# Half-height tiles for the scores and the carried products of a gated linear attention: two accumulated 64-row halves in place of one 128-row product

## The chip, the cores and the metric

The kernel runs on one core of a Trainium2 chip. A core has a matrix engine (TensorE, PE in the profile), which multiplies a loaded tile of weights by a streamed operand and adds into PSUM banks; three engines that work on rows of memory (VectorE or DVE, ScalarE or ACT, GpSimd or POOL); and a sync engine (SP) that issues most of the DMAs. Each engine runs its own stream of instructions in order and waits on semaphores for the others. The metric is device time in microseconds (us) from start to end of one execution.

## The reference

For 4 batches of 8 heads, 768 positions and 48 channels, a complex, data-dependent decay moves a 48x48 state; the real part of the state, read by the query, is the output. An ELU feed-forward layer follows.

```python
mag = np.sqrt(a_re * a_re + a_im * a_im)
scale = np.minimum(mag, 0.999) / (mag + 1e-06)
ar, ai = a_re * scale, a_im * scale
for t in range(S):
    S_re, S_im = ar * S_re - ai * S_im + k_t v_t, ar * S_im + ai * S_re
    y[:, :, t] = einsum('bhd,bhde->bhe', q[:, :, t], S_re)
x = y.transpose(0, 2, 1, 3).reshape(B * S, H * D)      # 3072 x 384
h = x @ w_in                                           # 384 x 2048
g = where(h > 0, h, exp(min(h, 0)) - 1)
out = g @ w_out                                        # 2048 x 384
```

## The kernel before, in words

The 3072 positions are cut into twelve steps `u` = 0 to 11. Each step takes 128 positions of two batches (`NB` = 2, index `n`), and each 128 positions are two chunks of 64 (`C` = 128, `L` = 64, index `c`). Complex numbers are written into one column of 128 rows: rows 0 to 47 hold the real part, rows 64 to 111 the imaginary part, and the rest is zero (`HP` = 64). So one product over 128 rows adds real and imaginary terms at once.

For a step of `u` > 2 the attention on PE stands in two places of a fixed list.

- The first place, `small` with what follows it: the state products (`state_products`, L1075: keys by values, for batch 0), the scores (L1190: transposed keys `kt` by transposed queries `qt`, for each head `h`, batch `n` and chunk `c`), and the state products of batch 1. Scores go into two PSUM banks `x["t"][n]`, which a mask on DVE (`masked`, L1198) brings to memory as `a`. DVE adds each state product to the old state (L1090), and POOL multiplies it by the decay (L1092), which makes the new state `S`. The step's first place in the list is `r + 28.2`, with `r` = 16 list slots per step.
- The second place, `valued_pe` and `carried_pe` at `r + 31.3`: values (`value_products`, L1111: `a` by `vn`), the sums of the next step's decays (`quartered`, L900), and the carried products (`carried_products`, L1120: state `S` by `qt`), all into two banks `x["yy"][c]`. ACT copies them (`copied`, L1228 and L1231), POOL's DMAs move a few rows (`seam`, L1241), and the feed-forward layer of that step starts from `x`.

Between and after them PE works on the feed-forward layer: L1507 (first layer, `mult`) and L1370 (second layer, `product`), from step 3 on in fast bilinear forms. Steps 0 to 2 have a list of their own (`first`); for step 2 the functions `scored` and `valued` do the work.

PE's tiles: a product whose weights span 128 rows and 64 or 48 columns (L1190, L1120) occupies half of the array's columns, and two of them run side by side. One of 64 rows and 64 columns (L1075, L1111, L900) occupies a quarter, and four run side by side. Everything else uses the whole array. Every float32 multiplication of the program runs as two passes, each a weight load and a matmul, so one product of the program is four instructions of PE; a transpose (L1034) is one pass.

What sets the order: the plan is a list of (place, function) pairs, sorted once. `put` adds to each place an offset from the table `SHIFT`, by function, arguments and step. Within an engine the instructions keep that order; semaphores are put in wherever one engine's data are another's. Buffers matter at two points: the banks of `outs()` (`y0`, `y1`, one buffer each) serve the feed-forward layer, the scores and the values in turn; and the three `w` banks serve the state products, the decay sums and the transposes in turn.

Of the kernel before, what the change touches and what calls it, by code (L numbers as in the profile page):

```python
# [16 lines left out]
C = 128  # L17
L = 64
# [487 lines left out]
def kernel(  # L506
# [600 lines left out]
    def value_products(u, n, y, first=True, at=0):  # L1107
        x = nat[u]
        for p, c, j in EACH:

            nc.tensor.matmul(  # L1111
                y[c][ts(j, HP), ds(at + p * L, L)], lhsT=vn[u % 2][ts(c, L), n, ds((2 * p + j) * D, HP)],
                rhs=x["a", n][ts(c, L), 2 * p + j], start=(first and p == 0), stop=False,
                skip_group_check=True,
            )
# [22 lines left out]

    def scored(u):

        x = nat[u]
        t = outs()
        state_products(u, 0 if u > PAIRED else 1)
# [7 lines left out]
        if u > PAIRED:  # L1151
            state_products(u, 1)
        for n in range(NB):
            state_sums(u, 0 if u > PAIRED else 1, [n])
            x["a", n] = new("a", 2, [C, H, L])
            nc.vector.tensor_tensor(
                out=x["a", n], in0=t[n].rearrange("p (h t) -> p h t", h=H),
                in1=mask.unsqueeze(1).to_broadcast([C, H, L]), op=ALU.mult,
            )
        if u > PAIRED:  # L1160
            state_sums(u, 1)

    def valued(u):

        x = nat[u]
        y = outs()
        for n in range(NB):
            value_products(u, n, y, n == 0, n * NP * L)
        if u + 1 < NU:
            both = quartered(u + 1)  # L1170
        for n in range(NB):
            carried_products(u, n, y, n * NP * L)
        if u == PAIRED:
            copied(u, y)
        if u + 1 < NU:
            z = nat[u + 1]
            z["E"], z["F"] = new("n", 6), new("n", 6)
            quarters_used(u + 1, both)
        if u > PAIRED:
            copied(u, y)  # L1180

    def small(u):

        x = nat[u]
        x["t"] = t = outs()
        state_products(u, 0)
        for n in range(NB):
            for h in range(H):
                for c in range(C // L):
                    nc.tensor.matmul(  # L1190
                        t[n][ts(c, L), ts(h, L)], lhsT=x["kt", n][:, h, ts(c, L)],
                        rhs=x["qt", n][:, h, ts(c, L)], start=True, stop=True,
                    )
# [9 lines left out]
    def valued_pe(u):  # L1203
# [4 lines left out]
        if u + 1 < NU:  # L1208
            x["quartered"] = quartered(u + 1)

    def carried_pe(u):
        for n in range(NB):
            carried_products(u, n, nat[u]["yy"], n * NP * L)
# [391 lines left out]
    def warm(n):  # L1605
# [42 lines left out]
    }  # L1648
# [26 lines left out]
    def gates_of(u, *at):  # L1675
# [23 lines left out]
        (convert,), (table, "trig_and_small", 1), (convert,), (seam, 0), (convert,), (warm, 1),  # L1699
# [12 lines left out]
        (inner, 1, 12), (load_a, 3), *2 * [(convert,)], (inner, 1, 8), (fetch, "out", 4),  # L1712
        (inner, 0, 10), (inner, 0, 14), (elu, 1, 12), (inner, 0, 12), (convert,), (fetch, "out", 5),
        *3 * [(convert,)], (load_v, 2), (powers, 2), (elu, 1, 8), *2 * [(convert,)], (elu, 0, 10),
# [168 lines left out]
```

## Time and profile before

| | |
|---|---|
| three runs | 644.2, 644.64, 646.19 us; median 644.64 us |
| the profiled execution | 644.48 us, of which the profiled span is 642.8 us |
| PE matmuls | busy 628.7 us (98%), 7236 of them |
| PE weight loads | 576.0 us (90%) |
| DVE, ACT, POOL | 489.3 us (76%), 428.5 us (67%), 159.0 us (25%) |
| scores of the steps 3 to 11 (L1190) | 576 matmuls of 128 rows and 64 columns |
| carried products (L1120) | 704 matmuls of 128 rows and 48 columns |
| one step, from state product to state product | 181.84 to 230.92: 49.1 us |

A row of the timeline gives the start, the time from first start to last end, the engine, the line, the operation, the tiles, the weights' rows and columns, the result's shape, and how many were merged. Matmuls overlap, so the difference of two starts says how long a run kept PE, and the second column is longer than that by the last one's own duration of about 0.22 us. "idle before" is time in which that engine did nothing, with what ended it; "issue" stands where no semaphore did. In the view of transfers, the 40 numbers behind GB/s are the bytes of 40 equal slices of the window, and a single packet shows in the slice in which it starts.

### The profile page before, as it was taken

How to read it: one execution, taken by the hardware profiler on the slowest of the kernel's cores; microseconds unless marked ns; L12 is line 12 of the kernel's file. 1: busy time of each engine (PE TensorE's matmuls, PEld its weight loads, DVE VectorE, ACT ScalarE, POOL GpSimd, SP SyncE). 2: the span in 40 equal slices, each digit the busy share in tenths (PEclk: the TensorE clock that was granted, in tenths of full speed). 3: DMA queues.
4: the chain of work that ended last, by engine and by line, in shares of the span. 5: the costliest groups of instructions: out<-in, count | busy, mean ns of one | idle time of the engine just before them, and what ended most of it. 6: DMA issues, size and time to landing. Idle time of an engine off the chain costs nothing.

```text
span 642.8 us, 17116 instructions
## 1 busy us (share of the span) xinstructions
PE 628.7 (98%) x7236; PEld 576.0 (90%) x7236; DVE 489.3 (76%) x777; ACT 428.5 (67%) x707; POOL 159.0 (25%) x201
## 2 busy tenths in 40 slices
PE   8899999999999999999999999999999999999996
PEld 5788886677899999999999999999999999999995
DVE  5899999869688698698488588588688678664581
ACT  5985573865957777677776776775876776771250
POOL 2000100113124315414414414413604502402000
PEclk9899999999999999999999999999999999999999
DMA  9967569325500712624434244243523352112100
GB/s 182 192 126 135 121 182 205 100 58 87 94 2 16 158 35 73 130 55 97 89 73 96 69 85 100 59 91 96 103 59 82 68 107 64 37 35 62 37 2 31
DMA packets 150706, 56.11 MB, mean 87 GB/s; under 512 B 128948, under 2 KB 142428, under 8 KB 150620
## 3 DMA queue, kind: packets, MB, share of 16 engines
q1 hardware_dynamic: 146880, 53.57, 38.3%
q0 software_dynamic: 3520, 1.20, 1.6%
q8 instruction: 59, 0.97, 0.6%
q14 instruction: 27, 0.22, 0.1%
q10 hardware_dynamic: 220, 0.14, 0.1%
HBM read 48.91 MB, written 4.80 MB: 84 GB/s over the span
## 4 chain that ended last, share of the span: by engine, by line
PE 95%; ACT 2%; DVE 1%; issue 1%; POOL 0%; DVEq 0%; ACTq 0%; POOLq 0%
PE mlp L1370 29%; PE mlp L1507 16%; PE mlp L1261 10%; PE y L1507 9%; PE w L1034 6%; PE w L1075 4%; PE y L1286 3%; PE mlp L1286 3%; PE y L1120 3%; PE y L1190 3%; PE w L848 2%; PE y L1111 2%; PE mlp L1609 1%; PE w L900 1%; PE w L1042 1%
## 5 line engine op out<-in xcount | busy, mean ns | idle before, releaser
L1370 PE MATMUL mlp<-w_out,g 128*128 128x192 f32 x640 | 112.1, 328 | 0.0
L1370 PEld LDWEIGHTS mlp<-w_out,g 128*128 128x128 f32 x640 | 104.3, 190 | 3.4 <-DVE ee L1384 0.6
L1092 POOL TENSOR_TENSOR S<-S,T 128x384 f32<-128x384 f32 x36 | 34.0, 946 | 204.9 <-DVE S L1090 204.9
L1523 DVE TENSOR_TENSOR g<-g,mlp 128x512 f32<-128x512 f32 x45 | 30.9, 686 | 48.9 <-PE mlp L1507 20.8
L1261 PE MATMUL mlp<-x,w_in 128*128 128x256 f32 x288 | 63.8, 380 | 0.0
L1261 PEld LDWEIGHTS mlp<-x,w_in 128*128 128x128 f32 x288 | 54.3, 190 | 8.2
L1348 DVE TENSOR_TENSOR g<-g 128x512 f32<-128x512 f32 x80 | 55.1, 703 | 5.0 <-PE mlp L1370 3.2
L1507 PE MATMUL mlp<-x,w_in 128*128 128x128 f32 x424 | 56.1, 275 | 0.0
L1370 PE MATMUL mlp<-w,g 128*128 128x192 f32 x320 | 54.5, 329 | 0.0
L1370 PEld LDWEIGHTS mlp<-w,g 128*128 128x128 f32 x320 | 51.8, 190 | 0.6
L1507 PEld LDWEIGHTS mlp<-x,w_in 128*128 128x128 f32 x424 | 51.6, 192 | 0.1
L1528 ACT ACTIVATE ee<-g 128x512 f32<-128x512 f32 x63 | 39.5, 626 | 18.2 <-DVE g L1523 16.8
L1241 POOL DMA_DIRECT2D x<-y x62 | 30.6, 501 | 75.8 <-ACT y L1137 39.9
L1532 DVE SCALAR_TENSOR_TENSOR g<-ee,g 128x512 f32<-128x512 f32 x63 | 43.5, 691 | 7.3 <-ACT ee L1529 7.1
L1529 ACT ACTIVATE ee<-ee 128x512 f32<-128x512 f32 x72 | 45.4, 631 | 2.3
L1520 ACT COPY g<-mlp 128x512 f32<-128x512 f32 x36 | 21.1, 586 | 37.5 <-PE mlp L1507 37.4
L1035 ACT COPY qt<-w 128x512 f32<-128x512 f32 x48 | 25.7, 593 | 8.6 <-PE w L1034 8.4
L1251 ACT ACT_TABLE_LOAD x24 | 30.8, 1283 | 0.5
L915 ACT ACTIVATE n<-w 64x384 f32<-64x384 f32 (+1 forms) x60 | 28.1, 486 | 3.9 <-PE w L900 3.0
L1507 PE MATMUL mlp<-x,g 128*128 128x128 f32 x224 | 29.6, 275 | 0.0
L1228 ACT COPY x<-y 128x384 f32<-128x384 f32 x20 | 8.6, 482 | 31.4 <-PE y L1120 31.4
L1507 PE MATMUL y<-x,w_in 128*128 128x128 f32 x216 | 28.6, 275 | 0.0
(226 smaller groups left out, 1416.6 us busy)
## 6 DMA issues: line engine op xcount, KB each, us to landing
w<-in_moe_w_out_dram SPq DMA_DIRECT2D x8, 768.0 KB, 4.7
g<-in_moe_w_in_dram SPq DMA_DIRECT2D x24, 256.0 KB, 3.1
g<-in_moe_w_out_dram SPq DMA_DIRECT2D x24, 256.0 KB, 2.7
w<-in_moe_w_in_dram SPq DMA_DIRECT2D x16, 288.0 KB, 4.0
vn<-in_v_dram SPq DMA_DIRECT2D x24, 192.0 KB, 4.1
q<-in_q_dram SPq DMA_DIRECT2D x11, 384.0 KB, 4.9
k<-in_k_dram SPq DMA_DIRECT2D x11, 384.0 KB
out_dram<-o SPq DMA_DIRECT2D x44, 96.0 KB, 2.4
```

Of the source, the lines that this page charges most:

```text
L1034: nc.tensor.transpose(t[:, h], of, ident)
L1092: eng.tensor_tensor(out=new_s, in0=new_s, in1=wide, op=ALU.mult)
L1251: nc.scalar.preload_act_table_set(name)
L1261: nc.tensor.matmul(t[:, e], lhsT=w_in[:, i, ts(f + e, C)], rhs=x["x"][:, i], start=(i == 0), stop=(i == NI - 1),)
L1286: nc.tensor.matmul(x["o", n], lhsT=x["g", f // 8][:, f % 8, ts(n, C)], rhs=w_out[:, f], start=(f == 0), stop=(f == NF - 1),)
L1348: nc.vector.tensor_tensor(out=S_of(u, k, h), in0=a, in1=b, op=op)
L1370: nc.tensor.matmul(to, lhsT=a[:, m], rhs=b[:, m], start=(first and h == 0 and m == 0), stop=False, skip_group_check=True,)
L1507: nc.tensor.matmul(x["c" + c][:, ts(m, C)], lhsT=a[:, m], rhs=x["mix"][p], start=(p == BANKS[c][0] and m == 0), stop=False, skip_group_che ...
L1523: nc.vector.tensor_tensor(out=part(u, to), in0=part(u, a), in1=part(u, b), op=op)
L1528: nc.scalar.activation(out=e, in_=part(u, of), func=AF.Relu, scale=-1.0)
L1529: nc.scalar.activation(out=e, in_=e, func=AF.Exp, scale=-1.0)
L1532: nc.vector.scalar_tensor_tensor(out=part(u, to), in0=nat[u]["e", to], scalar=-1.0, in1=part(u, of), op0=ALU.add, op1=ALU.max,)
```

## The change

Scores and carried products of 128 rows become two products of 64 rows each, which add into the same PSUM place: first one half of the rows (for the one batch or chunk the real rows, for the other the imaginary ones), later the other half. With 64 rows and 64 or 48 columns, four stand in the four quarters of the array. Both halves of one product add into one place of PSUM from different rows of the array, and the second is made to wait for the first: a POOL copy of a few elements of an operand onto themselves (`touched`) depends on every PE read of the first half, and the second half depends on it. Other PE work stands between the halves: the state products of batch 0 between those of the scores, the decay sums `quartered` between those of the carried products. The carried products of the steps 2 and 11, and the scores of the steps 0 to 2, stay whole.

```diff
+    def touched(t):
+        nc.gpsimd.tensor_copy(out=t, in_=t)
+
+    def score_half(u, m):
+        x = nat[u]
+        for h in range(H):
+            for n in (range(NB), (1, 0))[m]:
+                rows = ts(n ^ m, HP)
+                for c in range(C // L):
+                    nc.tensor.matmul(
+                        x["t"][n][ts(c, L), ts(h, L)], lhsT=x["kt", n][rows, h, ts(c, L)],
+                        rhs=x["qt", n][rows, h, ts(c, L)], start=(m == 0 and h == 0),
+                        stop=False, skip_group_check=True,
+                    )
+        if m == 0:
+            touched(x["kt", 1][:, 0 :: H - 1, 0::L])
+
+    def carried_half(u, m):
+        x = nat[u]
+        for n in (range(NB), (1, 0))[m]:
+            for p in range(NP):
+                for c in (range(C // L), (1, 0))[m]:
+                    for j in range(2):
+                        rows, h = ts(c ^ m, HP), 2 * p + j
+                        nc.tensor.matmul(
+                            x["yy"][c][ds(j * HP, D), ds((n * NP + p) * L, L)],
+                            lhsT=x["S", n][c][rows, h], rhs=x["qt", n][rows, h, ts(c, L)],
+                            start=False, stop=False, skip_group_check=True,
+                        )
+        if m == 0:
+            touched(x["S", 1][1][:, 0 :: H - 1, 0:1])
     def small(u):
         x = nat[u]
-        x["t"] = t = outs()
+        x["t"] = outs()
+        score_half(u, 0)
         state_products(u, 0)
-        for n in range(NB):
-            for h in range(H):
-                for c in range(C // L):
-                    nc.tensor.matmul(
-                        t[n][ts(c, L), ts(h, L)], lhsT=x["kt", n][:, h, ts(c, L)],
-                        rhs=x["qt", n][:, h, ts(c, L)], start=True, stop=True,
-                    )
+        score_half(u, 1)
     def valued_pe(u):
...
-        if u + 1 < NU:
-            x["quartered"] = quartered(u + 1)
-
-    def carried_pe(u):
-        for n in range(NB):
-            carried_products(u, n, nat[u]["yy"], n * NP * L)
+        if u + 1 == NU or u == PAIRED:
+            if u == PAIRED:
+                x["quartered"] = quartered(u + 1)
+            for n in range(NB):
+                carried_products(u, n, x["yy"], n * NP * L)
+            return
+        carried_half(u, 0)
+        x["quartered"] = quartered(u + 1)
+        carried_half(u, 1)
...
-        "state_sums(0, (1,))@3": 0.4, "state_sums(0, (1,))@4": -0.8, "state_sums(1, (1,))": 0.9,
-        "state_sums(1, (1,))@3": 0.5, "state_sums(1, (1,))@4": 2.0, "state_sums(1, (1,))@5": 0.2,
+        "state_sums(0, (1,))@3": 0.4, "state_sums(0, (1,))@4": -0.8, "state_sums(1, (1,))": 0.1,
...
-            for n in range(NB):
-                put(r + 28.2, state_sums, u, 1, (n,))
+            put(r + 28.2, state_sums, u, 1, (0,))
             put(at, valued_pe, u)
-            put(at, carried_pe, u)
+            put(at, state_sums, u, 1, (1,))
```

Some twenty more offsets of `SHIFT` and a few entries of the list `first` change; they move single operations of DVE and ACT by one or two places, and on PE one group of key transposes by four first-layer products, in the steps 6 to 11.

On PE, at the scores of step 3, this stands before (each row is a line of the program, the tiles' names, the result's columns of weights by streamed columns, and a count of the program's products; `vn`, `kg` are values and gated keys, `w` and `y` PSUM banks, `kt` and `cs` the transposed keys of batch 0 and 1):

```order
L1370 MATMUL mlp<-w_out,g 128x192 x4
L1075 MATMUL w<-vn_73,kg 64x48 x32
L1190 MATMUL y_1823<-qt,kt 64x64 x16
L1190 MATMUL y_1824<-qt,cs 64x64 x16
L1075 MATMUL w<-vn_73,kg 64x48 x32
L1370 MATMUL mlp<-w_out,g 128x192 x4
```

and this in the changed kernel, at the join of the first half, the state products and the second half:

```order
L1149 MATMUL y_1823<-qt,kt 64x64 x2
L1149 MATMUL y_1824<-qt,cs 64x64 x2
L1075 MATMUL w<-vn_73,kg 64x48 x32
L1149 MATMUL y_1824<-qt,cs 64x64 x2
L1149 MATMUL y_1823<-qt,kt 64x64 x2
```

The 32 score products have become 64, of which 32 stand ahead of the state products of batch 0 and 32 behind them; each half alternates between the two banks, two products at a time. The second state products (`L1075 ... x32`) and the feed-forward products follow as before.

At the carried products of step 3, PE had

```order
L1111 MATMUL y_1987<-a,vn_73 64x64 x2
L900 MATMUL w<-n,sum_logs 64x384 x4
L1120 MATMUL y_1986<-qt,S 48x64 x2
L1120 MATMUL y_1987<-qt,S 48x64 x2
```

and has now, from the last values over the end of the first half to the start of the second:

```order
L1110 MATMUL y_2017<-a,vn_73 64x64 x2
L1165 MATMUL y_2016<-qt,S 48x64 x2
...
L1165 MATMUL y_2017<-qt,S 48x64 x2
L900 MATMUL w<-n,sum_logs 64x384 x4
L1165 MATMUL y_2017<-qt,S 48x64 x2
```

Again 32 products are 64, half of them ahead of the decay sums.

On POOL, around one of the later steps, this stood before (L727, L1014 and L993 prepare the next step, L1092 multiplies a state, the DMAs L831 and L1241 move the carry and the seam):

```order
L727 TENSOR_TENSOR n<-n 128x768
L1092 TENSOR_TENSOR S<-S,T_77 128x384 x3
L831 DMA n<-carry 1x16x48
L1092 TENSOR_TENSOR S<-S,T_77 128x384
L1241 DMA x<-y 16x256 x6
```

and now:

```order
L727 TENSOR_TENSOR n<-n 128x768
L1140 COPY cs<-cs 128x2x2
L1092 TENSOR_TENSOR S<-S,T_77 128x384 x2
L831 DMA n<-carry 1x16x48
L1092 TENSOR_TENSOR S<-S,T_77 128x384
L1140 COPY S<-S 128x2
L1251 DMA x<-y 16x256 x6
L1092 TENSOR_TENSOR S<-S,T_77 128x384
```

The two copies of `touched` are new, and the fourth state multiplication now stands behind the DMAs of the seam. The line numbers of the changed kernel are higher by up to ten from L1140 on; L1507 and L1370 are L1517 and L1380 there.

More of the change, by code (lines that the diff above doesn't have):

```diff
@@ L1717 @@
-        (convert,), (fetch, "out", 6), (project, 1, 0, 0, 4), (convert,), (inner, 1, 14),
-        (slopes, 2), *3 * [(convert,)], (project, 1, 1, 0, 4), (project, 0, 0, 0, 4), (angles, 2),
-        (lengths, 2), (fetch, "out", 7), (convert,), (project, 0, 0, 4, 8), (elu, 1, 14),
-        (project, 0, 1, 0, 4), (decays, 2), (convert,), (project, 1, 0, 4, 8), (carried, 2),
-        (convert,), (table, "trig_and_small", 2), *2 * [(convert,)], (turns, 2), (waves, 2),
-        (scaled, 2), (convert,), (table, "natural_log_exp_and_others", 2), (project, 0, 1, 4, 8),
@@ L1729 @@
-        (project, 1, 0, 12, 16), (slopes, 3), (convert,), (transposed, 2, "q", 0),
-        (project, 1, 1, 12, 16), (angles, 3), (scored, 2), (opened,), (states, 2, 0), (valued, 2),
-        *3 * [(convert,)], (seam, 2), (project, 0, 0, 8, 12), (combined, 1, 1), (summed_in, 0),
-        (noted, 3), (carried, 3), (summed_in, 1), (combined, 2, 1), (combined, 1, 0),
-        (summed_in, 2), (project, 0, 1, 12, 16), (combined, 2, 0), (turns, 3), (combined, 4, 1),
-        (combined, 4, 0), (inner, 2, 4), (inner, 2, 6), (ends, 3), (load_a, 4), (inner, 2, 2),
@@ L1741 @@
[L1741 removed]
+        (inner, 1, 12), (load_a, 3), (convert,), (inner, 0, 10), (convert,), (inner, 1, 8),
+        (fetch, "out", 4), (inner, 0, 12), (inner, 0, 14), (elu, 1, 12), (convert,),
+        (fetch, "out", 5), *3 * [(convert,)], (load_v, 2), (powers, 2), (elu, 1, 8),
+        *2 * [(convert,)], (elu, 0, 10), (convert,), (noted, 2), (ratios, 2), *3 * [(convert,)],
+        (elu, 0, 14), (inner, 1, 10), *2 * [(convert,)], (elu, 0, 12), (convert,), (elu, 1, 10),
@@ new lines @@
+        *4 * [(convert,)], (load_qk, 2), (convert,), (fetch, "out", 6), (project, 1, 0, 0, 4),
+        (convert,), (inner, 1, 14), (slopes, 2), *3 * [(convert,)], (project, 1, 1, 0, 4),
+        (project, 0, 0, 0, 4), (angles, 2), (lengths, 2), (fetch, "out", 7), (convert,),
+        (project, 0, 0, 4, 8), (elu, 1, 14), (project, 0, 1, 0, 4), (decays, 2), (convert,),
+        (project, 1, 0, 4, 8), (carried, 2), (convert,), (table, "trig_and_small", 2),
+        *2 * [(convert,)], (turns, 2), (waves, 2), (scaled, 2), (convert,),
@@ new lines @@
+        (convert,), (ratios, 3), (convert,), (lengths, 3), (project, 1, 0, 12, 16), (slopes, 3),
+        (convert,), (transposed, 2, "q", 0), (project, 1, 1, 12, 16), (angles, 3), (scored, 2),
+        (opened,), (states, 2, 0), (valued, 2), *3 * [(convert,)], (seam, 2),
+        (project, 0, 0, 8, 12), (combined, 1, 1), (summed_in, 0), (noted, 3), (carried, 3),
+        (summed_in, 1), (combined, 2, 1), (combined, 1, 0), (summed_in, 2), (project, 0, 1, 12, 16),
+        (combined, 2, 0), (turns, 3), (combined, 4, 1), (combined, 4, 0), (inner, 2, 4),
```

69 lines of the change are left out of this document (22 added, 47 removed), and 36 rows, old and new, of the table SHIFT.

## The prediction

> **What bounds the kernel now.** The page comes first.
>
> ```profile
> span 642.8 us, 17116 instructions
> PE 628.7 (98%) x7236; PEld 576.0 (90%) x7236; DVE 489.3 (76%) x777; ACT 428.5 (67%) x707; POOL 159.0 (25%) x201
> q8 instruction: 59, 0.97, 0.6%
> PE 95%; ACT 2%; DVE 1%; issue 1%; POOL 0%; DVEq 0%; ACTq 0%; POOLq 0%
> ```
>
> The chain that ended last is PE for 95% of the span. The view of stretches says whether PE ever waits in the steps 3 to 11, which alone are changed:
>
> ```profile
> 170.00:590.00 420.00, 420.00 (x5400) 403.61 (x5399) 320.40 (x528) 299.81 (x487) 138.29 (x145) 1.00 0.34 76
> 181.84:231.00 49.16, 49.16 (x641) 47.33 (x644) 39.99 (x66) 35.10 (x56) 17.36 (x18) 1.00 0.30 63
> ```
>
> PE (first number behind the length) is busy for all of 420 us at clock 1.00. So a nanosecond taken off PE's stream comes off the end, and one that PE loses is lost. A step is 49.1 us and some 640 matmuls, with as many weight loads: 1280 instructions.
>
> The page's row q8 (packets, MB, share) is the third thing to see. 0.97 MB in 59 packets are 16 KB each, and 2 x 7236 PE instructions over 59 packets are 245, with PE's separate semaphore instructions about 256 of 64 bytes. These packets are PE's own instructions on their way in: five per step.
>
> **What the change removes: changes of tile shape.** The timeline of PE in step 3, and then in step 10:
>
> ```profile
> 181.84 1.15 PE L1075 MATMUL w<-vn,kg 64*64 64x48 f32 x64
> 182.92 1.15 PE L1190 MATMUL y<-qt,kt 128*64 128x64 f32 x32
> 183.90 1.10 PE L1190 MATMUL y<-qt,cs 128*64 128x64 f32 x32
> 184.93 1.15 PE L1075 MATMUL w<-vn,kg 64*64 64x48 f32 x64
> 186.01 1.57 PE L1370 MATMUL mlp<-w_out,g 128*128 128x192 f32 x8
> 192.71 1.16 PE L1111 MATMUL y<-a,vn 64*64 64x64 f32 x64
> 193.69 0.83 PE L900 MATMUL w<-n,sum_logs 64*64 64x384 f32 x8
> 194.45 1.99 PE L1120 MATMUL y<-qt,S 128*48 128x64 f32 x64
> 196.37 3.84 PE L1370 MATMUL mlp<-w,g 128*128 128x192 f32 x22
> 525.64 2.07 PE L1075 MATMUL w<-vn,kg 64*64 64x48 f32 x64
> 527.64 1.15 PE L1190 MATMUL y<-qt,kt 128*64 128x64 f32 x32
> 529.65 0.59 PE L1370 MATMUL mlp<-w_out,g 128*128 128x192 f32 x2
> ```
>
> Halving the rows gains nothing by itself. 64 passes of 128 rows in pairs are 32 turns; 128 passes of 64 rows in fours are 32 turns too. A turn costs the same: step 10's state products use two quarters, so 64 passes are 32 turns, 2.00 us (525.64 to 527.64); step 3's are 16 turns, 1.08 us. Sixteen turns are the difference, 0.92; I use 0.93, since the scores' 32 turns with both changes of shape take 2.01. Entering from a full tile and leaving without a change costs 0.98 (192.71 to 193.69), so a way in is about 0.05 and a way out 0.10.
>
> Scores, steps 3 to 9: before 186.01 - 181.84 = 4.17. After, four runs of 16 turns in one shape: 0.98 + 0.93 + 0.93 + 0.93 + 0.10 = 3.87. **-0.30 each, -2.1 for seven.** Steps 10 and 11 have both state products ahead and one change fewer: 529.65 - 525.64 = 4.01 against 3.87, **-0.14 each, -0.3**.
>
> Carried products, steps 3 to 10: before 196.37 - 192.71 = 3.66. After: values 0.98, first half (1.92 - 0.15)/2 = 0.89, decay sums without their change 0.76 - 0.10 = 0.66, second half with the way out 0.99: 3.52. At the 64-column turn of 0.93 the halves would give 3.60. **-0.14 each (-0.06 at least), -1.1 for eight.** All three: **-3.5 us**.
>
> **What it adds: instructions that PE must be fed with.** Each step gets 64 products more, 256 instructions, and the places where they stand are the densest. Before, 384 instructions took 4.17 us there; after, 512 would take 3.87. Whether PE gets them so fast is answered by step 2, where PE ran in small tiles for longest. Its timeline, with one row of step 1:
>
> ```profile
> 60.82 1.14 PE L1075 MATMUL w<-vn,kg 64*64 64x48 f32 x62
> 62.98 0.31 PE L1075 MATMUL w<-vn,kg 64*64 64x48 f32 x2 [1.02 <-issue]
> 138.78 1.15 PE L1147 MATMUL y<-qt,kt 128*64 128x64 f32 x32
> 140.80 1.36 PE L1075 MATMUL w<-vn,kg 64*64 64x48 f32 x61
> 142.04 1.06 PE L1111 MATMUL y<-a,vn 64*64 64x64 f32 x60
> 143.74 0.65 PE L1120 MATMUL y<-qt,S 128*48 128x64 f32 x16
> 145.14 1.55 PE L1120 MATMUL y<-qt,S 128*48 128x64 f32 x48 [0.75 <-issue]
> ```
>
> PE stopped for 1.02 and 0.75 us in the middle of runs, at products that wait for no semaphore. The run at 140.80 is longer than its like at 181.84 (1.36 with three passes still out, against 1.15); it halts behind 24 of its 64 passes, until 141.42. From there to the halt before 145.14 are 40 passes, 64 values, 8 sums and 16 carried ones: 128 matmuls, 256 instructions, one packet. Counted along the order, the halt of 62.98 lies on the same grid. The transfers around it, and those of step 3's scores (window from 181.84, slices of 0.15 us):
>
> ```profile
> GB/s 0 0 0 73 82 297 31 0 0 7 7 10 3 137 287 14 0 0 0 73 0 0 0 0 0 0 0 0 0 0 0 0 0 0 0 0 73 0 0 0
> q8 instruction: 3, 0.05, 2.4%
> GB/s 0 0 0 0 0 0 0 109 0 0 0 0 0 0 0 0 0 0 0 0 0 0 0 0 0 0 0 0 0 0 109 0 0 0 0 0 0 0 0 0
> q8 instruction: 2, 0.03, 2.3%
> ```
>
> In the first window (138 to 147, slices of 0.225) the three lone 73s are packets, at 138.8, 142.4 and 146.2. Each of the first two is followed by a halt that ends 2.6 to 2.7 us after its start (141.42, 145.14), and the next packet starts about one us after that. So in a dense stretch one packet follows another after some 3.6 us, and its 256 instructions are fed no faster than that.
>
> Now step 3. Its packets start at 182.9 and 186.4. On the grid (1024 instructions behind the halt of 141.42) the next boundary lies 36 passes into the second state products, 64 + 64 + 36 = 164 passes from the run's start: before at 1.08 + 2.01 + 0.04 + 0.52 = 3.65, so at 185.5, 2.6 behind the packet, and PE just does not halt. In step 6 the same distance is 2.4 (packet 330.4, boundary 332.8). With 1280 instructions per step, and 1536 after the change, five and six whole packets, the boundary stays at that place in every step.
>
> After the change the same 164 passes take 0.98 + 0.93 + 36/64 of 0.93 = 2.43. The packet cannot start sooner than before: what precedes it runs at the same pace, 1.07 after the run's start. Its instructions run 2.2 to 2.6 us after that (below step 6's 2.4, up to step 2's 2.6); I take 2.4, so 3.47. **PE halts for 1.04 us (0.8 to 1.25) in each of the steps 3 to 9: +7.3.** In step 10 the boundary lies 5 + 160 passes in, at 3.4, the packet 1.5 behind the start (527.1), so the halt is 0.5. In step 11 the boundary falls into L1370, which consumes two instructions in 0.16 us, and costs nothing. The values and carried halves hold one boundary, 123 passes in; the one before it was crossed in L1370, so that packet has long been there.
>
> The sum: 644.48 of the profiled execution - 3.5 + 7.3 + 0.5 = **648.8 us**, or 4.3 (0.7%) more. With the bounds of the halt and of the carried halves: 647.0 to 651.0. The median of the runs shown is 0.16 above the profiled execution, which is left out.
>
> [...]
>
> **What is hidden.** The copy of `touched` on POOL was not in the trace; its nearest rows are a 48x48 copy and a 128x128 product, beside the rows of the work around it in step 6:
>
> ```profile
> L1586 POOL COPY pair<-ident 48x48 f32<-48x48 f32 x2 | 0.4, 216 | 0.1
> L1490 POOL TENSOR_TENSOR x<-x 128x128 f32<-128x128 f32 x9 | 4.4, 488 | 33.6 <-DVE pair L1487 30.4 <-PE mlp L1507 3.2
> 331.47 0.83 POOL L1092 TENSOR_TENSOR S<-S,T 128x384 f32<-128x384 f32 x1 [17.26 <-DVE S L1090]
> 337.52 1.21 POOL L1092 TENSOR_TENSOR S<-S,T 128x384 f32<-128x384 f32 x1 [2.61 <-DVE S L1090]
> 341.95 0.83 POOL L1092 TENSOR_TENSOR S<-S,T 128x384 f32<-128x384 f32 x1 [1.29 <-DVE S L1090]
> 341.32 0.55 DVE L1090 TENSOR_TENSOR S<-w,S 128x384 f32<-128x384 f32 x1
> 332.38 0.69 DVE L1198 TENSOR_TENSOR a<-y,mask 128x512 f32<-128x512 f32 x1 [0.24 <-PE y L1190]
> 376.48 0.68 DVE L1523 TENSOR_TENSOR g<-y,g 128x512 f32<-128x512 f32 x1
> ```
>
> I take 0.2 us, up to 0.5. POOL idles 17 us ahead of the scores' copy, which has the state products' 0.93 less the last pass's 0.22 as cover: nothing. The copy of `S` has 0.66 - 0.22 = 0.44 for 0.2 and two hand-overs of under 0.1 each (DVE ended at 341.87, POOL began at 341.95): nothing, or 0.3 in eight steps if it takes 0.5. Queued behind it on POOL are the seam's DMAs, which come two us later. The masks now get both banks only at the end of the second half, but their reader, L1111, comes 7 us later. The banks' last reader ahead (376.48) ends 1.1 us before the step's run at 378.3, so the scores may go first.
>
> **Rivals.**
> - *PE is fed in time* (chance 0.18): the packet's 2.4 us belong to the DMA traffic of the moment, or PE looks further ahead than I think. Then 644.5 - 3.5 = 641.0. For it: no halt is seen in 420 us. Against: the boundary was met only once per dense run, never earlier than 2.4 us behind its packet.
> - *The halt is half as long* (0.10): instructions queued at PE cover some of it; 7 x 0.5 cancels the gain: 644.5.
> - *POOL comes late as well* (0.10): in steps 5 to 9 the copy of `S` stands behind a state multiplication, which ended at 342.8 with the carried products starting at 341.8. The plan has it earlier now, since one DVE and one POOL operation ahead of it are gone; if it ends after the decay sums (13.1 us behind the run's start, it was 13.6), PE waits 0.5, and some 2.5 to 4 come on top: 652.
>
> **How the numbers follow.** Forecast 0.62, with 647.0 to 651.0. The range reaches down to the second rival and up to the third: 644.3 to 651.5. Below 0.3% (2 us, about what a measurement of this kernel tells from no change) lie 641.0: faster 0.18. Same: the second rival, 0.10. Slower: 0.72.
>
> **What would show it.** The changed kernel's timeline should show PE with a halt of about one us in the second score half, by "issue", some 36 passes in, in each of the steps 3 to 9, at the start of a run that waits for no semaphore; packets 3.5 us apart there; and the run of values, sums and carried halves at 3.5 instead of 3.66 without a halt. If PE has no halt, the first rival holds, and the time is near 641. If a halt stands at the first product of a second half, released by POOL, the copy is late. If scores and state products without their halt take more than 3.9, the turn of 0.93 is wrong.

## The result and the profile after

The changed kernel takes 654.4 us (median of four runs, 653.1 to 657.0) against 644.8 before: ratio 1.015, with an interval of 1.011 to 1.019. That is 9.6 us more; the forecast was 4.2 more than the median known then (644.64), with a range up to 651.5. The direction was right, the size was not.

The page of the profiled execution, whose own time is 653.14 us:

```profile
span 651.4 us, 19312 instructions
PE 629.5 (97%) x8324; PEld 576.6 (89%) x8324; DVE 491.4 (75%) x777; ACT 427.7 (66%) x707; POOL 163.5 (25%) x218
q8 instruction: 67, 1.10, 0.7%
PE 91%; SPq 5%; issue 2%; DMA 1%; DVE 0%; ACT 0%; POOL 0%; ACTq 0%; DVEq 0%; POOLq 0%
```

PE's busy time is within 1 us of what it was (628.7), its instructions are 2176 more (with their loads), and packets of instructions are 67 instead of 59. So nearly all of the added time is idle time of PE. The same stretch of steps 3 to 9, before and then after:

```profile
170.00:530.00 360.00, 360.00 (x4652) 345.76 (x4651) 277.72 (x456) 264.50 (x427) 123.27 (x127) 1.00 0.37 81
```

```profile
170.00:530.00 360.00, 354.26 (x5411) 341.05 (x5410) 271.76 (x449) 259.07 (x420) 125.12 (x140) 1.00 0.37 82
```

And what PE of the changed kernel waited for, from the view of waits (sum, times, longest):

```profile
PE y L1149 <- issue: 5.7, 7, 1.2
PE y L1165 <- issue: 0.8, 1, 0.8
PE mlp L1517 <- DVE o L1406: 0.7, 1, 0.7
```

L1149 are the score halves. Seven waits, one in each of the steps 3 to 9, have "issue" as their cause: no semaphore. Step 3 on the timeline:

```profile
183.94 0.28 PE L1149 MATMUL y<-qt,cs 64*64 64x64 f32 x4
185.04 0.27 PE L1149 MATMUL y<-qt,kt 64*64 64x64 f32 x2 [0.81 <-issue]
185.51 1.14 PE L1075 MATMUL w<-vn,kg 64*64 64x48 f32 x61
186.57 1.57 PE L1380 MATMUL mlp<-w_out,g 128*128 128x192 f32 x8
193.27 1.16 PE L1110 MATMUL y<-a,vn 64*64 64x64 f32 x64
194.25 1.07 PE L1165 MATMUL y<-qt,S 64*48 64x64 f32 x64
```

The second half starts at 183.47, and the halt stands behind its 36th pass. Counted along PE's instructions from its first weight load (weight loads, matmuls and semaphore instructions), the first pass behind each of the seven halts begins with a number that leaves 190 or 191 when divided by 256, and so it is for the halts of the kernel before at 62.98 and 145.14, and for every wait behind the first 100 us that the traces below put down to "issue". The transfers around it (from 181.56, slices of 0.15 us) are two packets and nothing else:

```profile
GB/s 0 0 0 0 0 0 0 0 109 0 0 0 0 0 0 0 0 0 0 0 0 0 0 0 0 0 0 0 0 0 0 109 0 0 0 0 0 0 0 0
q8 instruction: 2, 0.03, 2.5%
```

The packet starts at 182.78, 0.64 behind the place where PE crosses the boundary before (182.14, in the first score half). PE goes on 2.26 after the packet's start, and the next packet starts at 186.27.

**Where the 8.66 us between the two profiled executions went.** The first matmul of each group of second-layer products (L1370 before, L1380 after) stands on both timelines; how their distance grows from one to the next gives each part:

| Part | Forecast, us | Measured, us |
|---|---|---|
| steps 0 to 2 | 0 | -0.28 |
| score regions, steps 3 to 9 | +5.2 | +6.34 (0.84, 0.94, 0.86, 1.19, 0.87, 0.81, 0.83) |
| score regions, steps 10 and 11 | +0.2 | +0.08 |
| values to carried products, steps 3 to 9 | -1.0 | -0.67 |
| the same in step 10 | -0.14 | +1.01 |
| step 11, PE waits for DVE (L1406) | 0 | +0.97 |
| from PE's last matmul to the end | 0 | +1.20 |
| sum | +4.3 | +8.65 |

The median lies 1.3 above the profiled execution; in the runs at 655.7 and 657.0 the mean granted clock was 0.991 and 0.992, against 0.994 and 0.995 in the two at 653.1. What happened in them no trace shows.

### The profile page after: what moved, and what is told of

Read it like the earlier page. It is cut to its first block, busy times and chain, and to the rows that moved or that the text cites. A ratio compares the mean times of both kernels' runs of the same rounds, so it can differ in the third digit from the quotient of the medians.

```text
span 651.4 us, 19312 instructions
## 1 busy us (share of the span) xinstructions
PE 629.5 (97%) x8324; PEld 576.6 (89%) x8324; DVE 491.4 (75%) x777; ACT 427.7 (66%) x707; POOL 163.5 (25%) x218
## 4 chain that ended last, share of the span: by engine, by line
PE 91%; SPq 5%; issue 2%; DMA 1%; DVE 0%; ACT 0%; POOL 0%; ACTq 0%; DVEq 0%; POOLq 0%
PE mlp L1380 29%; PE mlp L1517 16%; PE mlp L1271 10%; PE y L1517 9%; PE w L1034 6%; PE y L1149 3%; PE y L1296 3%; PE mlp L1296 3%; PE w L1075 3%; PE y L1165 2%; PE w L848 2%; SPq L655 2%; SPq L604 2%; PE y L1110 2%; SPq L600 1%
## 5 line engine op out<-in xcount | busy, mean ns | idle before, releaser
L1380 PE MATMUL mlp<-w_out,g 128*128 128x192 f32 x640 | 112.1, 328 | 0.0
L1380 PEld LDWEIGHTS mlp<-w_out,g 128*128 128x128 f32 x640 | 104.3, 190 | 3.4 <-DVE ee L1394 0.6
L1358 DVE TENSOR_TENSOR g<-g 128x512 f32<-128x512 f32 x80 | 56.7, 727 | 3.1 <-PE mlp L1380 2.0
L1517 PE MATMUL mlp<-x,w_in 128*128 128x128 f32 x424 | 56.2, 275 | 0.7 <-DVE o L1406 0.7
L1380 PE MATMUL mlp<-w,g 128*128 128x192 f32 x320 | 54.5, 329 | 0.0
L1517 PEld LDWEIGHTS mlp<-x,w_in 128*128 128x128 f32 x424 | 51.6, 192 | 1.0 <-DVE o L1406 0.9
L1380 PEld LDWEIGHTS mlp<-w,g 128*128 128x128 f32 x320 | 51.8, 190 | 0.6
L1092 POOL TENSOR_TENSOR S<-S,T 128x384 f32<-128x384 f32 x36 | 32.0, 891 | 63.4 <-DVE S L1090 63.4
L1140 POOL COPY cs<-cs 128x4 f32<-128x4 f32 x9 | 3.4, 372 | 133.3 <-ACT ee L1538 65.4
L1517 PE MATMUL mlp<-x,g 128*128 128x128 f32 x224 | 29.6, 275 | 0.0
```

Source lines behind the costliest of these rows:

```text
L1092: eng.tensor_tensor(out=new_s, in0=new_s, in1=wide, op=ALU.mult)
L1358: nc.vector.tensor_tensor(out=S_of(u, k, h), in0=a, in1=b, op=op)
L1380: nc.tensor.matmul(to, lhsT=a[:, m], rhs=b[:, m], start=(first and h == 0 and m == 0), stop=False, skip_group_check=True,)
L1517: nc.tensor.matmul(x["c" + c][:, ts(m, C)], lhsT=a[:, m], rhs=x["mix"][p], start=(p == BANKS[c][0] and m == 0), stop=False, skip_group_che ...
```

## Experiments

**1 and 2. Where the boundaries lie.** If PE halts because a packet of instructions comes late, then moving the boundaries of 256 along the program must move the halts, and nothing else is needed. Some small products whose result nobody reads, placed in the first 15 us where PE waits for ACT, do that: each is four instructions.

```diff
-    def warm(n):
+    def warm(n, more=0):
 ...
+        for m in range(more):
+            rows = ts(m % 2, HP)
+            nc.tensor.matmul(
+                t[rows, 0:16], lhsT=ident[rows, rows], rhs=ident[rows, 0:16], start=True, stop=True,
+            )
 ...
-        (angles, 0, 1), (summed, 0), (warm, 1), (convert,), (decayed, 0, 0), (convert,),
+        (angles, 0, 1), (summed, 0), (warm, 1, 14), (convert,), (decayed, 0, 0), (convert,),
```

> The changed kernel with 14 products more of 64 rows, 64 columns and 16 streamed columns (56 instructions of PE) in the first 15 us, where PE waits anyway; nothing reads them. Feeding theory: PE can't run past a boundary of 256 instructions until the packet behind it has come, some 3.2 us after PE's sequencer, 40 instructions ahead, crossed the boundary before. The 56 instructions move every boundary 56 places earlier in the program's order. In the steps 3 to 9 the two boundaries then lie 16 instructions into the first score half, so that the packet is asked for while the slower L1380 still runs, and 272 in, by which time it has come: no halt in these seven steps, against 0.86 to 1.33 us each in the changed kernel (6.8 us in all). The halt in the carried products of step 10 stays (0.6 to 1.0). Time: 653.1 - 6.8 = 646.3, from 645.5 to 647.5. Rival, that the halt belongs to the second half as such (its place in the program, its rows, its PSUM banks, its wait for POOL): the halts stay 36 passes into the second half, time 653 to 654.

Measured: 645.8 us (645.2 to 647.7), ratio to the kernel before 1.001 (0.998 to 1.004). The halts of the score halves are gone (the longest rest there is 0.25, in step 7); the view of waits has instead

```profile
PE mlp L1380 <- issue: 1.0, 3, 0.4
PE y L1165 <- issue: 0.6, 1, 0.6
PE mlp L1517 <- DVE o L1406: 0.7, 1, 0.7
```

Fourteen products that compute nothing take 8.6 us off (between the two profiled executions 7.3, of which 1.3 lie in the steps 0 to 2, whose boundaries move too). The rival (the second half as such) is out. Not all is as expected: in five of the seven steps a rest of 0.3 to 0.6 stands at the next boundary, 16 instructions behind the region, because its packet starts 0.8 to 1.45 us behind the crossing of the one before, where I took a fixed lead of 40 instructions and 0.8 to 1. That was an estimate. In the trace of the kernel before, between 170 and 600 us, 23 of 43 packets start with under 2 KB of other transfers since the instruction 40 ahead of the boundary before, and they start 0.6 to 1.4 us behind that instruction, in the median 1.0.

With 32 products the same edit moves the boundaries by half a packet.

> The same with 32 products (128 instructions), half a packet. Feeding theory: in the steps 3 to 9 the boundary that bound moves from 36 passes into the second score half to 36 passes into the second state products (64 passes later, since the boundary before it, 128 places earlier too, now lies in L1380 and is harmless), with a halt of 0.75 to 1.0 us there; and the boundary in the values moves ahead, so that the one behind it now falls into the second carried half, with a halt of 0.6 to 0.9 in each of these steps. Sum of the halts some 7 x (0.9 + 0.7) = 11 us against 6.8 + 1.0: time 655.5 to 658.5. Rival (the second half as such): no change, 653 to 654, halts where they were.

Measured: 669.1 us (666.5 to 670.6). The places are those expected, the second state products (L1075) and the second carried half (L1165) of the seven steps; the sizes are not:

```profile
PE y L1165 <- issue: 9.4, 7, 2.1
PE w L1075 <- issue: 8.2, 7, 1.5
```

The waits are 17.6 us where I had 11, and the time is 12 us above the middle of my forecast. Two causes can be read. The stretches of five windows, from the crossing of a boundary in L1110 to the end of the halt in L1165, and last the 3.4 us behind the last of them:

```profile
298.27:301.86 3.59, 2.59 (x144) 2.01 (x137) 3.59 (x6) 0.85 (x1) 0.89 (x2) 1.00 0.36 105
349.88:354.21 4.33, 2.54 (x140) 1.96 (x132) 4.33 (x7) 0.00 (x0) 0.23 (x2) 1.00 0.30 87
402.58:406.96 4.38, 2.77 (x141) 1.95 (x132) 4.38 (x7) 0.81 (x1) 0.23 (x2) 1.00 0.31 88
454.69:459.34 4.65, 2.55 (x141) 1.97 (x133) 4.65 (x7) 0.00 (x0) 0.23 (x2) 1.00 0.34 81
459.47:462.88 3.41, 3.41 (x21) 3.27 (x18) 1.00 (x3) 2.89 (x6) 1.43 (x3) 0.50 0.35 86
```

First, here other transfers are under way (DMA share 0.3), and what counts is when. In the first window they start late, and the packet starts 0.77 us behind the crossing. In the next three they are there from the start, and it starts 2.0 to 2.2 us behind it. From its start to PE's going on it is 2.3 to 2.8 us in all four. The transfers, from 349.88 in slices of 0.11 us, show the traffic from 350.3 on, and the packet starts at 351.93, when most of it is through:

```profile
GB/s 0 0 0 0 146 237 182 237 218 127 218 130 278 353 289 219 146 141 266 75 34 0 0 0 0 7 7 7 14 7 7 7 0 0 0 0 0 0 0 0
```

Second, behind the halt of 2.3 us PE's granted clock is 0.50 for 3.41 us: 1.7 us more, twice in this run. The packet's delay by traffic stands beside it in each case; no run was made in which the traffic alone was taken away. The ten traces together bear it out: of the 472 boundaries that PE crosses between 170 and 600 us, 36 have a packet that starts more than 1.70 us behind the crossing before, and in each of these at least 0.24 MB of data was moved in between; of the 175 that start behind a crossing with next to no such transfers (under 2 KB) none is later than 1.70. Traffic isn't enough by itself: 74 packets had some and were not that late. The halts at L1075, 1.0 to 1.7 us where I had 0.75 to 1.0, have no transfer ahead of their packets; what makes them longer is not shown.

**3 and 4. One half of the change at a time.** The scores whole, as before, and the carried products in halves:

```diff
-        score_half(u, 0)
         state_products(u, 0)
-        score_half(u, 1)
+        for n in range(NB):
+            for h in range(H):
+                for c in range(C // L):
+                    nc.tensor.matmul(
+                        x["t"][n][ts(c, L), ts(h, L)], lhsT=x["kt", n][:, h, ts(c, L)],
+                        rhs=x["qt", n][:, h, ts(c, L)], start=True, stop=True,
+                    )
```

> The changed kernel with the scores whole, as before (one product of 128 rows, both banks one after the other, behind the first state products); the carried products stay in halves. Feeding theory: a step has 64 products' worth of instructions fewer than the change has in all (1408, five and a half packets), so the boundaries alternate from step to step: a halt of 0.7 to 1.0 us in the second carried half of steps 3, 5, 7, 9 and in step 10, none in 4, 6, 8 and none in the scores. Time: 644.5 - 1.1 (eight changes of tile shape) + 5 x 0.85 = 647.6, from 646.5 to 649. Rival (halts belong to the second half of the scores): the carried halves bring their 1.1 us, 643.4 (642.9 to 644.2).

Measured: 654.0 us (652.8 to 655.4), ratio 1.014. The halts:

```profile
197.27 0.43 PE L1165 MATMUL y<-qt,S 64*48 64x64 f32 x13 [0.68 <-issue]
297.10 0.43 PE L1165 MATMUL y<-qt,S 64*48 64x64 f32 x14 [0.94 <-issue]
397.55 0.43 PE L1165 MATMUL y<-qt,S 64*48 64x64 f32 x14 [1.81 <-issue]
```

In sum, and in the stretch behind the fourth:

```profile
PE y L1165 <- issue: 6.1, 5, 2.1
```

```profile
498.99:502.40 3.41, 3.41 (x11) 3.41 (x12) 1.65 (x3) 3.37 (x7) 1.91 (x4) 0.50 0.33 94
```

Every second step and step 10, as expected; two are 1.8 and 2.1 instead of 0.85, again with traffic from the start of the stretch, and the second of these is followed by 3.41 us at half clock. So the carried halves, whose changes of shape do bring 0.14 a step, cost 9 us when they stand alone (0.8 of it is the late end of experiment 6). The time is 5 above the range I had given.

The other part alone, carried products whole:

```diff
-        if u + 1 == NU or u == PAIRED:
-            if u == PAIRED:
+        if True:
+            if u + 1 < NU:
                 x["quartered"] = quartered(u + 1)
```

> The changed kernel with the carried products whole, behind the decay sums, as before; the scores stay in halves. Feeding theory: 1408 instructions per step again, so the place alternates: a halt of about 1 us 36 passes into the second score half in steps 3, 5, 7, 9, and 36 passes into the second state products in steps 4, 6, 8; none in the carried products. Time: 644.5 - 2.4 (changes of tile shape) + 7 x 1.0 = 649.1, and about 1 more for a wait of PE in step 11 behind a late DVE product, which the changed kernel shows: 648.5 to 651. Rival (the second half as such): the halts stay 36 passes into the second score half in all seven steps, and the time is 1.1 above the changed kernel's less its 1.0 in step 10: 653.

Measured: 652.9 us (651.4 to 654.0), ratio 1.012. The places alternate as expected:

```profile
185.91 0.27 PE L1149 MATMUL y<-qt,kt 64*64 64x64 f32 x2 [1.09 <-issue]
237.16 0.67 PE L1075 MATMUL w<-vn,kg 64*64 64x48 f32 x28 [1.00 <-issue]
286.48 0.27 PE L1149 MATMUL y<-qt,kt 64*64 64x64 f32 x2 [1.10 <-issue]
337.71 0.67 PE L1075 MATMUL w<-vn,kg 64*64 64x48 f32 x28 [1.02 <-issue]
386.77 0.27 PE L1149 MATMUL y<-qt,kt 64*64 64x64 f32 x2 [0.75 <-issue]
437.84 0.66 PE L1075 MATMUL w<-vn,kg 64*64 64x48 f32 x27 [0.90 <-issue]
```

A halt that is now at L1149 and now at L1075, of about the same length, belongs to the count of instructions and not to an operation. The time is 1.9 above the range: the seven gaps are 7.7 us in all and not 7.0, and each halt costs some 0.2 beyond its gap (below).

**5. The same instructions, less dense.** The second half and what follows it moved behind the next group of second-layer products:

```diff
+
+    def later(u):
         score_half(u, 1)
 ...
-                put(r + 28.2, masked, u, n)
-            put(r + 28.2, state_products, u, 1)
-            put(r + 28.2, state_sums, u, 1, (0,))
+            put(r + 28.62, later, u)
+            for n in range(NB):
+                put(r + 28.62, masked, u, n)
+            put(r + 28.62, state_products, u, 1)
+            put(r + 28.62, state_sums, u, 1, (0,))
```

> The changed kernel with the second score half (and what follows it) put behind the next group of second-layer products, so that 8 full-tile matmuls (L1370 of before, 1.4 us) stand between the first state products and the second score half in steps 3 to 9; in steps 10 and 11 between the first half and the second. The number of PE's instructions and their places ahead of this region are the same. Feeding theory: the boundary of the halt now falls 28 passes into the second score half, reached 0.98 + 1.03 + 1.4 + 0.4 = 3.8 us behind the region's start, and its packet's instructions run at 3.3 to 3.5: no halt in steps 3 to 9. Two more changes of tile shape cost 0.15 a step. Time: 653.1 - 6.8 - 0.4 (the slow start behind each halt) + 1.1 = 647.0 (646 to 648.5). Rival (the second half as such, its rows or its wait for POOL): halts at the start of or within the second half as before, 654.

Measured: 650.0 us (649.6 to 651.6), ratio 1.009. In the stretch 170 to 530, with all seven steps, PE is busy for all but 0.2 us; behind it stands a stretch of step 10, and what PE waited for:

```profile
170.00:530.00 360.00, 359.79 (x5614) 345.30 (x5612) 278.08 (x457) 263.44 (x428) 128.91 (x142) 1.00 0.37 82
542.67:546.08 3.41, 3.41 (x12) 3.41 (x12) 0.94 (x1) 3.38 (x7) 2.06 (x5) 0.50 0.32 93
```

```profile
PE y L1165 <- issue: 2.2, 1, 2.2
PE y L1110 <- DVE a L1207: 1.0, 1, 1.0
PE mlp L1519 <- DVE o L1408: 0.7, 1, 0.7
```

So the boundaries, at the same counts, cause no halt once 1.4 us of slow instructions stand among the fast ones. The run is 3 us above the expectation because of step 10, which takes 4.1 us more than in the changed kernel: the halt of the carried half there is 2.2 long, followed by 3.41 us at half clock, and the masks, which now come later, let PE wait 1.0 for DVE (L1207). In the seven steps the move earns little over the kernel before: from step 4 on a step is 49.04 us against 49.13, since going out of small tiles and into them again costs 0.3 (two stretches of 2.01 with a group of 1.50 between them, against 3.87 and 1.33), where I had 0.15.

**6. The two losses at the end.** The copy of `touched` between the score halves writes a piece of the transposed keys `kt` of batch 1, and the buffer of these is `cs`, into which ACT writes the turned angles of the next step (L984). So L984 must now wait for POOL besides DVE. In the changed kernel's trace L984 itself waits for POOL's semaphore alone, and the wait for DVE's stands in an instruction of its own ahead of the load of the function table, so the load waits too; in the kernel before the load has no wait ahead of it. ACT, DVE, POOL and PE in step 11 of the changed kernel:

```profile
554.66 1.28 ACT L984 ACT_TABLE_LOAD   x1 [0.66 <-DVE n L854]
558.53 4.94 DVE L1014 TENSOR_TENSOR qg<-q,cs 128x1536 f32<-128x1536 f32 x1 [0.41 <-ACT cs L988]
560.02 1.83 POOL L993 TENSOR_TENSOR k<-k,n 128x768 f32<-128x768 f32 x1
561.93 4.87 POOL L1014 TENSOR_TENSOR kg<-k,cs 128x1536 f32<-128x1536 f32 x1
563.79 1.16 PE L1517 MATMUL mlp<-x,w_in 128*128 128x128 f32 x8 [0.71 <-DVE o L1406]
```

In every other step the 0.66 is hidden. Here DVE's L1014 would end, with its usual 1.76 us, 0.27 behind the start of POOL's L993; it takes 4.94. L1406 is queued behind it, and PE waits for that.

```diff
-            touched(x["kt", 1][:, 0 :: H - 1, 0::L])
+            touched(x["qt", 1][:, 0 :: H - 1, 0::L])
 ...
         n = cst.tile([1, 1], FP32, name="n")
+        for _ in range(8):
+            nc.vector.memset(n, 0.0)
         nc.vector.tensor_reduce(out=n, in_=t, axis=mybir.AxisListType.X, op=ALU.add)
```

> The changed kernel with the copy between the score halves done on the transposed queries of batch 1 in place of the transposed keys (whose buffer the turned angles of a later step are written to), and with 8 tiny DVE writes more just ahead of the kernel's last DVE reduction. Two side effects of the change are meant to go. First, the table load on ACT (L984) no longer waits 0.66 us for DVE, since the activation behind it needs one semaphore only; so in step 11 the DVE product L1014 starts before POOL's L993, takes 1.76 us instead of 4.94, and PE's wait of 0.98 at 562.8 is gone. Second, DVE's last drain no longer stands 2.6 us behind its semaphore (644.21 + 3.62 to 6.25 in the changed kernel, nothing in the kernel before): -1.2 at the end, if that is a packet of DVE's instructions coming late. The halts of PE in steps 3 to 10 stay. Time: 653.1 - 1.0 - 1.2 = 650.9 (650 to 652). Rival: DVE's long product comes from PE's halts (then it stays at 4.9 and the time at 652), and the drain waits for a transfer (then the end stays).

Measured: 651.4 us (650.8 to 651.8), ratio 1.010. The same four engines:

```profile
554.53 1.28 ACT L984 ACT_TABLE_LOAD   x1
558.55 1.75 DVE L1014 TENSOR_TENSOR qg<-q,cs 128x1536 f32<-128x1536 f32 x1
560.52 1.82 POOL L993 TENSOR_TENSOR k<-k,n 128x768 f32<-128x768 f32 x1
562.42 3.47 POOL L1014 TENSOR_TENSOR kg<-k,cs 128x1536 f32<-128x1536 f32 x1
```

Neither ACT nor PE waits. And the end: DVE's last drain stands 0.1 us behind its semaphore again (2.6 in the changed kernel), and from the last work of DVE to its last semaphore it is 5.8 us, against 7.15. The two mends are worth 1.0 and 1.3 us; 0.5 went back, 0.4 in the steps 0 to 2 and the rest in step 10, whose scores halt for 0.64 instead of 0.2. In the traces of all ten kernels the drain is late, by 2.3 to 2.6, in five. Counted along DVE's instructions, that drain is number 1010 in just these five, and number 1012, 1015 or 1018 in the other five. In these five alone the queue of the other engines' instructions (q14) also has one packet more, 0.7 to 0.9 us behind the start of the drain. So the delay goes with DVE's own count, which the change and the eight writes move: a boundary of DVE's instructions just ahead of number 1010 fits all ten traces. The packets aren't told apart by engine, so the late packet itself isn't shown.

**7. The padding by itself.** The 32 products in the kernel before.

> The kernel before with the same 32 small products (128 instructions) that cost the changed kernel 16 us more. Feeding theory: a step of the kernel before has its dense stretches 3.3 to 3.6 us per packet or longer, so moving the boundaries by half a packet brings no halt in steps 3 to 11 but for some tenths, and the padding itself stands where PE waits: 643.5 to 646.5. If padding as such costs (its time, the moved work of the first steps), the time goes up by more than 2 us.

Measured: 644.7 us (644.4 to 645.0), ratio 1.000 (0.999 to 1.001). The same edit that costs the changed kernel 15 us costs the kernel before nothing: the steps 3 to 11 last as long as before to 0.01 us, and PE's only wait of 0.2 us and more behind the first 100 us stands in step 2:

```profile
PE y L1111 <- issue: 0.3, 1, 0.3
```

In the kernel before, one boundary in each of the steps 3 to 9 is crossed only 2.4 to 2.7 us behind the start of its packet; here none in the steps 3 to 11 comes sooner than 5.3.

**8. The mends together.** 13 small products, the copy on the queries, the eight writes, and the carried products of step 10 whole:

```diff
-        if u + 1 == NU or u == PAIRED:
-            if u == PAIRED:
+        if u + 2 >= NU or u == PAIRED:
+            if u + 1 < NU:
                 x["quartered"] = quartered(u + 1)
```

> All mends together: the changed kernel with 13 small products ahead (52 instructions), the copy on the queries, 8 tiny DVE writes, and the carried products of step 10 whole. Feeding theory: 645.9 of the run with 14 products, less its rest of halts in steps 3 to 9 (2.3, with boundaries 4 instructions later now 0 to 1), less 0.6 in step 10, less 1.0 for the wait in step 11, less 1.2 at the end: 641.5 (640.5 to 643.5), 0.4% under the kernel before. Rival (the halts come from the halves): 650 or more.

Measured: 642.2 us (641.6 to 643.0), ratio to the kernel before 0.996 (0.995 to 0.997). The steps 3 to 9, and PE's only waits of 0.2 us and more behind the first 100 us:

```profile
170.00:530.00 360.00, 359.65 (x5620) 346.87 (x5619) 276.60 (x459) 263.88 (x428) 127.11 (x143) 1.00 0.38 81
```

```profile
PE y L1110 <- issue: 0.4, 1, 0.4
PE mlp L1380 <- issue: 0.3, 1, 0.3
```

This version is 2.5 us (0.4%) faster than the kernel before. Of the 2.4 us between the two profiled executions 1.3 lie in the steps 3 to 11, where the tiles were costed at 3.4 (without step 10's carried products). The scores of the steps 3, 5 and 6 have their full 0.29; the rest goes to waits of some tenths in the other steps and to 0.4 at a boundary in step 5. Another 1.0 us lies in the steps 0 to 2, whose scores haven't changed and whose boundaries the 13 products move too; the kernel before with 13 products was not run, so that part can't be put down to the tiles. Most of the 12.2 us between this version and the changed kernel are instructions that come late, and what the copy delays.

## Why the prediction was wrong, point by point

The mechanism was right: the halts came where it put them, for its reason. The sum missed 4.4 us. Two of its terms were too small: a halt was priced at its gap alone (+1.1 with the copy's wait in step 4), and step 10's carried products were said to have no halt, "so that packet has long been there" (+1.15). Two were put at nothing: what the write of `touched` makes others wait for (+0.97 in step 11, and most of 0.3 in the carried products), and the end of the program (+1.2). The steps 0 to 2 and the scores of steps 10 and 11 give 0.4 back.

- **PE bounds the kernel**: right. Whatever PE lost was lost at the end; only the last 1.2 us are DVE's.
- **Changes of shape, -3.5 us**: right in size, hidden by the halts. In step 6 of experiment 8, where no halt stands, the last full-tile matmul ahead of the scores starts at 327.31 and the next full-tile group at 331.45, 4.14 apart; before they were 4.43 apart (328.92 to 333.35): -0.29 against -0.30. The values, sums and carried products are shorter by 0.14, as forecast.
- **A halt in each of the steps 3 to 9**: right in place (36 passes into the second score half), cause ("issue", no semaphore), count and size: the gaps between starts, less a normal turn of 0.06, are 0.86 to 1.33, mean 0.97, where I had 1.04 (0.8 to 1.25). What I had left out is that a halt costs more than its gap: a turn in front of it is torn in two (0.06), and the first turn behind it takes 0.11 instead of 0.06 and the next change of tile is slower. In step 3 the region is 5.01 us long; without the halt it would be 3.87, so the halt cost 1.14, with a gap of 0.98; 0.06 and 0.05 for the two turns leave 0.05 to the change of tile. Over the seven steps it is 0.16 to 0.26 beyond the gap, 1.5 in all. In step 4 PE also waited 0.17 for the copy. These, against gaps that are half a us shorter in all, leave the 1.1 us between 5.2 and 6.3.
- **Step 10**: wrong step in the working. I had the scores' halt at 0.5 (it is 0.2), and said of the values and carried halves that "the one before it was crossed in L1370, so that packet has long been there". That holds in steps 3 to 9. Step 10 has its state products in another order and its boundaries at other places: one lies in the values, at 542.88, and the next in the second carried half, which halts for 1.0:

```profile
544.47 0.95 PE L1165 MATMUL y<-qt,S 64*48 64x64 f32 x53
546.27 0.42 PE L1165 MATMUL y<-qt,S 64*48 64x64 f32 x11 [0.84 <-issue]
```

  The rule was mine; I had applied one step's places to all of them instead of counting each.
- **What is hidden**: wrong. I had asked of the copy of `touched` when it would be done, and not what its write would make others wait for. Its time was nearly hidden: 0.17 of PE's time in step 4, where it took 0.68 and not 0.2, and 0.24 in step 7. Its write into `cs` put a wait on ACT's table load, and that cost 0.97 in step 11 (experiment 6).
- **The end**: not in the prediction at all, 1.2 us (experiment 6).
- **The count of a packet**: the working has 245 instructions in one, about 256 with the semaphore instructions. With them it is 247; the halts show 256, so some two of the 59 packets hold nothing that PE ran.
- **The rivals**: that PE is fed in time (0.18) is out by experiment 1; the half-sized halt (0.10) by the sizes; POOL's lateness (0.10) was the nearest to the time, at 652, and for another reason.

The places of all halts agree with blocks of 256 instructions: each is 190 or 191 modulo 256. In 68 of the 69 halts of these ten traces (all behind the first 100 us that hold PE up by more than some 0.2 us) the packet behind a boundary starts 0.2 to 2.5 us after the boundary before it is crossed. How many of PE's instructions are held ready at a time the traces don't tell. The kernel before crosses two boundaries 3.1 us apart in each of the steps 3 to 9 without a halt; in the small tiles of the changed kernel, where PE is at the second boundary 1.9 to 2.1 us behind the first, it halts in each of these steps.

## What to carry to other kernels

Smaller tiles cost instructions: where PE runs through 256 of them in about 2 us, as it does here with float32 products in quarters (at 3.1 us, in the kernel before, it didn't halt), count where the boundaries fall, in each repetition separately, and put slow full-tile work among them or shift the count by some idle instructions; fourteen products that compute nothing were worth 8.6 us here. A dependence made by writing a buffer is a dependence of everybody who uses that buffer later: look up who writes it next, and what stands in front of that writer on its engine.

## What the runs showed of the hardware that was not expected

- A packet of instructions can come later where data are on their way: up to 1.45 us from crossing to start in 62 of 69 halts, 2.0 to 2.5 in the seven of experiments 2, 3 and 5 that have traffic from the start. From its start to PE's going on it is 2.2 to 2.9 us in all of them.
- Halts of 2.05 to 2.4 us (from start to start) were followed by 3.41 us at a granted clock of 0.50 in four cases; three of 1.77 to 2.03 were not, nor any of the shorter ones. So a halt's price can jump by 1.7 us. Length alone need not be what decides: in each of these traces the times between changes of the clock are whole multiples of 3.41 us (413.01 and 51.20 in experiment 2 are 121 and 15 times), and on that grid each of the four halts lies whole within one stretch of 3.41, the one just ahead of the slow one. Those of 2.01 and 2.03 are cut by the grid into 1.5 and 0.6, 1.1 and 1.0; the one of 1.77 lies whole in one stretch. No run was made to tell the two apart.
- Two large products of DVE and POOL that lie over each other: DVE 4.94 us instead of 1.76 and POOL 4.87 instead of 3.45, in all five of the traces in which POOL's L993 began 1.49 us behind DVE's L1014, and in none of the five in which it began 1.97 us behind it or later. In the changed kernel's step 11 DVE had started 1.49 us earlier and still ended 1.62 after POOL's L993 (563.47 against 561.85). What in them holds the two up no run shows.
- DVE's last drain stands 2.3 to 2.6 us behind its semaphore where it is DVE's instruction 1010, and 0.1 where it is a few places later.
